# Second MLP product by seven block products, with four sums a side instead of five and the combination done by accumulating in PSUM

## The chip, the cores and the metric

The kernel runs on one core of a Trainium2 chip. The metric is the device time of one execution in microseconds (us). A run also records the core's span from its first to its last instruction, which is some 1.8 us shorter than the time, and the mean granted clock of TensorE.

Names: PE is TensorE (matmuls), PEld its weight loads, DVE is VectorE, ACT is ScalarE, POOL is GpSimd, SP is the queue that issues most transfers. PSUM is the memory that matmuls write; the kernel has eight buffers in it, called banks here, each of the size of one matmul result of 128 x 512 in fp32. L587 means line 587 of that kernel; the same code has other line numbers before and after the change.

## The reference

Causal attention with decay, in blocks of 64 positions, and behind it an MLP with a gelu:

```python
for b in range(nb):                       # B=4, H=8, S=768, D=64; block 64
    intra = (qb @ kb.T * Dmask) @ vb
    inter = (qb * lam_pow) @ kv_state
    out[:, :, sl] = intra + inter
    kv_state = lam_block * kv_state + (kb * rev_pow).T @ vb
x = out.transpose(0, 2, 1, 3).reshape(B * S, H * D)       # 3072 x 512
h = x @ w_in                                              # 512 x 2048
g = 0.5 * h * (1 + tanh(c * (h + 0.044715 * h**3)))
return g @ w_out                                          # 2048 x 512
```

The change concerns the last line alone, `g @ w_out`.

## The kernel before

Attention runs in 24 steps. The MLP's work lies in a list `filler`, from which pieces are taken between the parts of the attention steps, so that TensorE always has something to do. The rows of the MLP go in seven groups: g = 0 has 512 rows and takes plain products, g = 1 and 2 have 256 rows, g = 3 to 6 have 512. From g = 1 on the second product splits activations and weights into 2 x 2 blocks and makes seven block products in place of eight. A block product is eight matmuls of 256 columns. The blocks are combined by sums on both sides (VectorE), and the products by adds (VectorE) behind copies (ScalarE):

```python
G_SUMS = {5: ((0, 0), ALU.add, (0, 1)), 2: ((1, 0), ALU.add, (1, 1)),
          1: ((0, 0), ALU.add, (1, 1)), 7: ((0, 1), ALU.subtract, (1, 1)),
          6: ((1, 0), ALU.subtract, (0, 0))}
PLACE = {4: ("A", 0), 3: ("A", 1), 5: ("B", 0), 2: ("B", 1), 1: ("C", 0), 7: ("D", 0), 6: ("D", 1)}

def product(m, p):
    ...
    for i in range(HF):
        ...
        pin(nc.tensor.matmul(dst, lhsT, rhs, start=(i == 0), stop=(i == HF - 1),
                             skip_group_check=True))
    if m == 2:
        ...
        pin(nc.scalar.activation(out=m525[:, 0:2], in_=B[:], func=AF.Copy))
        pin(nc.scalar.activation(out=m525[:, 2], in_=B[:, 0], func=AF.Copy))
        pin(tt(banks["diag"], A[:], m525[:, 0:2], ALU.subtract))
        pin(tt(flat[:, 1:3], A[:], m525[:, 1:3], ALU.add))
    elif m == 1:
        pin(tt(d, banks["C"][:, 0].unsqueeze(1).to_broadcast([P, 2, HE]), d, ALU.add))
    elif m == 6:
        pin(tt(d, banks["D"][:], d, ALU.add))
        # then two stores of 256 KB; in the last pair four of 128 KB, each as soon as it can go
```

Each product writes its half of a bank once and no product waits for a read in the middle of its own bank's life. `pin` keeps the program's order on each engine.

## Time and profile before

| what | value | where from |
|---|---|---|
| time | 204.34 us, median of 5 (203.80 to 204.52) | the runs |
| span of the profiled run | 202.2 us | the page |
| busy: PE, DVE, ACT | 194.2, 145.7, 107.9 us | the page, part 1 |
| PE in the chain that ended last | 81% | the page, part 4 |
| granted clock | 1.000 | the view of cores |
| last matmul starts, span ends | 198.54, 202.16 us | the trace |

The lines themselves stand in the prediction. Read them in this order. The busy table tells which engine has no room (PE) and which has some (DVE at 72%). The slices tell whether that holds throughout or only on average: DVE is at 9 tenths in eight slices in a row before the middle of the run and at 2 to 7 in its last fifth. The chain tells what the end waited for. Since a busy PE may still be slow, the last reading is the distance from one matmul's start to the next: 109 ns for 256 columns is its rate here, and anything above that is a hole. The holes are the only thing that a change can win back which leaves the matmuls alone.

### The profile page before, as it was taken

The page shows a single profiled execution, that of the slowest core. Times are in us where ns is not written, and L with a number is a line of the kernel's source. Part 1 is how long each engine was busy: PE and PEld are TensorE (multiplying, and loading weights), DVE is VectorE, ACT ScalarE, POOL GpSimd, SP SyncE. Part 2 cuts the span into 40 slices and gives each one's busy share as a digit, 9 for nine tenths or more (in the row PEclk, how much of TensorE's full clock was granted, in tenths as well). Part 3 has the DMA queues.
Part 4 walks back from the last instruction along what each step waited for, and adds up shares of the span by engine and source line. Part 5 has one row for each costly group of instructions (what it writes and reads, how often), then busy time and mean ns, then how long its engine had stood idle before and what let it go on. Part 6 is the DMA issues. An engine that isn't in the chain of part 4 may idle for free.

```text
span 202.2 us, 5666 instructions
## 1 busy us (share of the span) xinstructions
PE 194.2 (96%) x2348; PEld 130.1 (64%) x2348; DVE 145.7 (72%) x293; ACT 107.9 (53%) x205; POOL 66.3 (33%) x80
## 2 busy tenths in 40 slices
PE   6888999999999999999999999999999999999993
PEld 1456544456888888645688764589664688544882
DVE  5896623889999999967799749899566462334753
ACT  2475778375893473477642368614367424466210
POOL 6594123457458264162531609303302000000000
PEclk9999999999999999999999999999999999999999
DMA  5999999999999999999875999306510003300014
GB/s 170 291 327 387 387 387 378 286 291 320 334 239 216 272 233 235 210 277 200 205 182 127 243 285 218 45 0 138 132 51 3 0 0 107 104 0 0 3 45 163
DMA packets 64201, 37.85 MB, mean 187 GB/s; under 512 B 17584, under 2 KB 59568, under 8 KB 64176
## 3 DMA queue, kind: packets, MB, share of 16 engines
q1 hardware_dynamic: 63344, 36.97, 72.1%
q10 hardware_dynamic: 832, 0.52, 0.8%
q8 instruction: 18, 0.29, 0.6%
q14 instruction: 7, 0.06, 0.1%
HBM read 27.26 MB, written 6.29 MB: 166 GB/s over the span
## 4 chain that ended last, share of the span: by engine, by line
PE 81%; DVE 6%; SPq 4%; DMA 4%; ACT 2%; issue 2%; DVEq 0%
PE Hps L484 37%; PE MB L555 8%; PE MA L555 8%; PE MD L555 7%; SPq L70 4%; PE MC L555 4%; DMA wi<-in_moe_w_in_dram 4%; PE Hps L601 3%; PE O2ps L499 3%; PE S L295 3%; DVE w_sum L128 2%; PE OK L353 2%; PE OK L344 1%; PE Tps L266 1%; DVE gs L531 1%
## 5 line engine op out<-in xcount | busy, mean ns | idle before, releaser
L484 PE MATMUL Hps<-xT,w_in 128*128 128x512 f16 (+1 forms) x416 | 78.7, 346 | 0.0
L488 ACT ACTIVATE gT<-Hps 128x512 f16<-128x512 f32 x88 | 52.3, 597 | 29.1 <-PE Hps L484 28.3
L484 PEld LDWEIGHTS <-w_in 128*128 128x128 f16 x416 | 40.4, 98 | 33.7
L531 DVE TENSOR_TENSOR gs<-gT 128x1024 f16<-128x1024 f16 (+1 forms) x62 | 40.8, 712 | 18.3 <-ACT gT L488 18.3
L456 POOL TENSOR_TENSOR u<-t,lumask 128x256 f16<-128x256 f32 x40 | 29.4, 749 | 67.0 <-DVE t L449 49.6
L555 PEld LDWEIGHTS <-gs 128*128 128x128 f16 x400 | 39.0, 98 | 4.5
L305 DVE TENSOR_TENSOR PT<-S,mask 128x512 f16<-128x512 f32 x48 | 30.4, 682 | 9.5 <-PE S L295 9.5
L230 POOL TENSOR_TENSOR v<-v,dv 128x512 f16<-128x512 f32 x24 | 28.5, 1194 | 5.0 <-DMA v<-in_v_dram 4.5
L555 PE MATMUL MA<-w_sum,gT 128*128 128x256 f16 x160 | 19.5, 273 | 0.4 <-DVE o L587 0.3
L555 PE MATMUL MB<-w_out,gs 128*128 128x256 f16 x160 | 19.1, 273 | 0.0
L248 ACT ACTIVATE qk<-k 128x512 f16<-128x512 f32 x24 | 15.0, 625 | 7.6 <-DMA k<-in_k_dram 7.6
L562 ACT ACTIVATE m<-MB 128x512 f32<-128x512 f32 x10 | 6.0, 597 | 23.4 <-PE MB L555 23.4
L555 PE MATMUL MD<-w_sum,gs 128*128 128x256 f16 x152 | 18.4, 273 | 0.0
L555 PEld LDWEIGHTS <-gT 128*128 128x128 f16 x160 | 15.4, 98 | 3.5 <-ACT gT L488 0.5
L243 DVE TENSOR_TENSOR qk<-q,dq 128x512 f16<-128x512 f32 x23 | 17.6, 767 | 0.0
L430 ACT ACTIVATE xT<-OK 128x256 f16<-128x256 f32 x29 | 11.1, 453 | 8.2 <-PE OK L353 7.9
L499 PE MATMUL O2ps<-w_out,gT 128*128 128x512 f16 x64 | 14.6, 379 | 0.0
L566 DVE TENSOR_TENSOR o<-MA,m 128x512 f32<-128x512 f32 x10 | 6.9, 689 | 9.6 <-ACT m L562 9.6
L128 DVE TENSOR_TENSOR w_sum<-w_out 128x1024 f16<-128x1024 f16 x10 | 9.1, 947 | 6.3 <-POOL w_out L118 3.5
L430 ACT ACTIVATE xT<-O 128x256 f16<-128x256 f32 x18 | 6.4, 458 | 10.4 <-PE O L404 7.5
L295 PEld LDWEIGHTS <-qkT 64*64 64x64 f16 x384 | 6.0, 106 | 7.0 <-issue 3.2
L449 DVE SCALAR_TENSOR_TENSOR t<-t,lamu,OK 128x64 f32<-128x64 f32 x44 | 10.1, 273 | 0.5
(68 smaller groups left out, 168.8 us busy)
## 6 DMA issues: line engine op xcount, KB each, us to landing
q<-in_q_dram SPq DMA_DIRECT2D x24, 256.0 KB, 5.3
k<-in_k_dram SPq DMA_DIRECT2D x24, 256.0 KB, 5.2
v<-in_v_dram SPq DMA_DIRECT2D x23, 256.0 KB, 5.2
out_dram<-o SPq DMA_DIRECT2D x22, 256.0 KB, 4.5
wo<-in_moe_w_out_dram SPq DMA_DIRECT2D x4, 1024.0 KB, 9.6
wi<-in_moe_w_in_dram SPq DMA_DIRECT2D x4, 512.0 KB, 7.6
wi<-in_moe_w_in_dram SPq DMA_DIRECT2D x2, 1024.0 KB, 12.7
v<-in_v_dram ACTq DMA_DIRECT2D x1, 256.0 KB, 4.4
```

The source lines that it names most:

```text
L128: pin(eng.tensor_tensor(w_sum16[:, w_slot[m], 4 * j : 4 * j + 4, :], rows(f0, e0), rows(f1, e1), op))
L230: pin(nc.gpsimd.tensor_tensor(wide(tv[:]), ld32[s][2][:], decay(dv, s), ALU.mult))
L243: pin(q_eng.tensor_tensor(wide(tq), q32[:], decay(dq, s), ALU.mult))
L248: pin(nc.scalar.activation(out=wide(tk), in_=k32[:], func=AF.Copy))
L305: pin(nc.vector.tensor_tensor(t[:, hl].rearrange("p b c d -> p b (c d)"), Sps[:].rearrange("p b c d -> p b (c d)"), mask[:].unsqueeze(1).t ...
L430: pin(nc.scalar.activation(out=d, in_=o, func=AF.Copy))
L456: pin(nc.gpsimd.tensor_tensor(u[:], state[half][:].unsqueeze(2).to_broadcast([P, 2, 2, D]), lumask[:, 2 * half : 2 * half + 2, :].unsqueez ...
L484: pin(nc.tensor.matmul(by_block(Hps[:, i, :]), w_in16[:, c, f * P : (f + 1) * P], x(c), start=(c == 0), stop=(c == NC - 1)))
L488: pin(nc.scalar.activation(out=dst, in_=Hps[:], func=AF.Gelu_apprx_tanh))
L499: pin(nc.tensor.matmul(O2[tau][0][:], gT[:, f % HF, f // HF, tau * P : (tau + 1) * P], w_out16[:, f, :], start=(n == 0), stop=(n == NF - 1)))
L531: pin(nc.vector.tensor_tensor(gsum[m][:, i, :], block(T0, F0, i), block(T1, F1, i), op))
L555: pin(nc.tensor.matmul(dst, lhsT, rhs, start=(i == 0), stop=(i == HF - 1), skip_group_check=True))
```

## The change

With activation blocks Gij (i: half of the rows, j: half of the 2048) and weight blocks Wij, the new form is

```
S1 = G10+G11   S2 = S1-G00   S3 = G00-G10   S4 = G01-S2
T1 = W01-W00   T2 = W11-T1   T3 = W11-W01   T4 = W10-T2
P1 = G00*W00  P2 = G01*W10  P3 = S4*W11  P4 = G11*T4  P5 = S1*T1  P6 = S2*T2  P7 = S3*T3
out00 = P1+P2   out01 = P1+P6+P5+P3   out11 = P1+P6+P7+P5   out10 = P1+P6+P7+P4
```

Its intent is to take work off VectorE: four sums a side instead of five, and a combination that TensorE does itself by accumulating. Bank X takes products 1, 6, 7 and 4 one upon the other and is read between them; W takes product 2; Y takes 5 and then 3. The order is 1 2 5 6 3 7 4, for both row tiles of a group in turn. The price is that some sums are now made from other sums (S2 from S1, S4 from S2), and that TensorE has to wait until a bank has been read before it may go on in it. Each sum is issued by itself, behind a chosen product. Core of the diff:

```diff
-        G_SUMS = {5: ((0, 0), ALU.add, (0, 1)), ... five of them, each of two plain blocks
+        G_SUMS = {1: ((1, 0), ALU.add, (1, 1)), 2: (1, ALU.subtract, (0, 0)),
+                  3: ((0, 0), ALU.subtract, (1, 0)), 4: ((0, 1), ALU.subtract, 2)}
+        FACTORS = {1: ((0, 0), (0, 0)), 2: ((0, 1), (1, 0)), 3: (4, (1, 1)), 4: ((1, 1), 4),
+                   5: (1, 1), 6: (2, 2), 7: (3, 3)}
...
+        paired = HN // P == 2                     # groups of 512 rows
...
+                if m == 1:
+                    st["X"] = ps_M.tile([P, HE], FP32, tag="M", name="MX")[:]
+                elif m == 2 and paired:
+                    wy = ps_M.tile([P, 2, HE], FP32, tag="M", name="MWY")
+                    st["W"], st["Y"] = wy[:, 0], wy[:, 1]
...
+            opens = m in (1, 2) or (m == 5 and not paired)
+            closes = m in (2, 3, 4)
...
+            if m == 1:
+                copied("m1")                      # ScalarE, from X
+            elif m == 2:
+                added(0, 0, "m1")                 # VectorE, W + m1
+            elif m == 5:
+                copied("q")                       # ScalarE, from Y
+            elif m == 6:
+                copied("u2")                      # ScalarE, from X
+            elif m == 3:
+                added(1, 0, "u2")                 # VectorE, Y + u2
+                store(0)
+            elif m == 7:
+                added(1, 1, "q")                  # VectorE, X + q
+                if final:
+                    store(1, 1)
+            elif m == 4:
+                pin(nc.scalar.activation(out=o[:, 0, 1, :], in_=dst, func=AF.Copy))
+                store(1, 0 if final else None)
...
-        ms = ((3, 4, 5, 2), (1, 7, 6))
+        order = [(m, p) for m in (1, 2, 5, 6, 3, 7, 4) for p in range(HN // P)]
...
+            behind(5, 0, 4, (1, 2))
+            behind(6, 0, 4, (4, 3))
+            behind(7, 4, 8, (1,))
+            behind(8, 4, 8, (2,))
+            behind(9, 4, 8, (4,))
+            behind(10, 4, 8, (3,))
...
+    BURST = {18: (2, 5, 4), 20: (3, 10, 5), 22: (3, 6, 4)}
+    for n, (a, b, c) in BURST.items():
+        burst((n, n + 1), (17,) if n == 18 else (n - 2, n - 1))
+        fill(a)
+        U(n)                                      # state updates: VectorE, then GpSimd
+        U(n + 1)
+        if n + 3 < NSTEP:
+            prep(n + 3)                           # q scaling on VectorE, and more
+        fill(b)
...
```

The weight sums follow the same pattern (eight instructions instead of ten), and steps 16 and 17, which were one burst, become two single steps.

More of the change, by code (lines that the diff above doesn't have):

```diff
@@ L78 @@
     HF, HE = NF // 2, DM // 2
-    w_sum16 = w16p.tile([P, 5, HF, HE], FP16)
-    W_SUMS = {3: ((0, 1), ALU.subtract, (1, 1)), 4: ((1, 0), ALU.subtract, (0, 0)),
-              1: ((0, 0), ALU.add, (1, 1)), 7: ((1, 0), ALU.add, (1, 1)),
-              6: ((0, 0), ALU.add, (0, 1))}
+    w_sum16 = w16p.tile([P, 4, HF, HE], FP16)
+    W_SUMS = {1: ((0, 1), ALU.subtract, (0, 0)), 2: ((1, 1), ALU.subtract, 1),
+              3: ((1, 1), ALU.subtract, (0, 1)), 4: ((1, 0), ALU.subtract, 2)}
     w_slot = {m: i for i, m in enumerate(W_SUMS)}
@@ L120, in sum_wout, with rows @@
     def sum_wout(j, m, eng):
-        (f0, e0), op, (f1, e1) = W_SUMS[m]
-        def rows(f, e):
-            f = f * HF + 4 * j
-            return w_out16[:, f : f + 4, e * HE : e * HE + HE]
-        pin(eng.tensor_tensor(w_sum16[:, w_slot[m], 4 * j : 4 * j + 4, :], rows(f0, e0), rows(f1, e1), op))
+        a, op, b = W_SUMS[m]
+        r = slice(4 * j, 4 * j + 4)
+        def rows(t):
+            if t in w_slot:
+                return w_sum16[:, w_slot[t], r, :]
+            f, e = t
+            return w_out16[:, f * HF + r.start : f * HF + r.stop, e * HE : e * HE + HE]
+        pin(eng.tensor_tensor(rows(m), rows(a), rows(b), op))
     lam_in = const.tile([H, 1], FP32)
@@ L460, in update, with gs_tiles @@
             us[(s, c)] = u
+    gs_kept = []
+    def gs_tiles(g):
+        if g < 3:
+            if not gs_kept or gs_kept[0] != g:
+                gs_kept[:] = [g, wst.tile([P, 4, HF, P], FP16, tag="w32", name=f"gs_{g}")]
+        elif not gs_kept or gs_kept[0] < 3:
+            gs_kept[:] = [3] + [wst.tile([P, 2, HF, 2 * P], FP16, tag="w32", name=f"gs{i}")
+                                for i in range(2)]
+        return gs_kept[1:]
     groups = [[0, 1], [2], [3], [4, 5], [6, 7], [8, 9], [10, 11]]
@@ L510, in queue_group @@
         HN = N // 2
-        G_SUMS = {5: ((0, 0), ALU.add, (0, 1)), 2: ((1, 0), ALU.add, (1, 1)),
-                  1: ((0, 0), ALU.add, (1, 1)), 7: ((0, 1), ALU.subtract, (1, 1)),
-                  6: ((1, 0), ALU.subtract, (0, 0))}
-        G_PLAIN = {3: (0, 0), 4: (1, 1)}
-        W_PLAIN = {5: (1, 1), 2: (0, 0)}
-        gsum, pairs = {}, []
-        def block(T, F, i):
+        G_SUMS = {1: ((1, 0), ALU.add, (1, 1)), 2: (1, ALU.subtract, (0, 0)),
+                  3: ((0, 0), ALU.subtract, (1, 0)), 4: ((0, 1), ALU.subtract, 2)}
@@ L519, in block, with g_rows, sum_g @@
+        FACTORS = {1: ((0, 0), (0, 0)), 2: ((0, 1), (1, 0)), 3: (4, (1, 1)), 4: ((1, 1), 4),
+                   5: (1, 1), 6: (2, 2), 7: (3, 3)}
+        gsum = {}
+        def g_rows(t, i):
+            if t in G_SUMS:
+                return gsum[t][:, i, :]
+            T, F = t
             return gT[:, i, F, T * HN : (T + 1) * HN]
-        def sum_g(i0, i1, ms=None):
-            for m, ((T0, F0), op, (T1, F1)) in G_SUMS.items():
-                if ms and m not in ms:
-                    continue
+        def sum_g(i0, i1, ms):
+            for m in ms:
+                a, op, b = G_SUMS[m]
@@ L525, in sum_g @@
                 if m not in gsum:
                     k = len(gsum)
-                    if k % 2 == 0:
-                        pairs.append(wst.tile([P, 2, HF, HN], FP16, tag="w32", name=f"gs_{g}_{m}"))
-                    gsum[m] = pairs[-1][:, k % 2]
+                    held = gs_tiles(g)
+                    gsum[m] = held[0][:, k] if per == 2 else held[k // 2][:, k % 2]
                 i = slice(i0, i1)
-                pin(nc.vector.tensor_tensor(gsum[m][:, i, :], block(T0, F0, i), block(T1, F1, i), op))
+                pin(nc.vector.tensor_tensor(g_rows(m, i), g_rows(a, i), g_rows(b, i), op))
@@ L533, in queue_group @@
+        last_group = g == len(groups) - 1
+        paired = HN // P == 2
         of_pair = {}
-        PLACE = {4: ("A", 0), 3: ("A", 1), 5: ("B", 0), 2: ("B", 1), 1: ("C", 0), 7: ("D", 0),
-                 6: ("D", 1)}
-        def product(m, p):
-            banks = of_pair.setdefault(p, {})
-            name, half = PLACE[m]
-            final = g == len(groups) - 1 and p == HN // P - 1
-            if final and m == 6:
-                name = "E"
-            if m in (3, 5, 1, 7) or name == "E":
-                banks[name] = ps_M.tile([P, 2, HE], FP32, tag="M", name=f"M{name}")
-            dst = banks[name][:, half]
-            t = slice(p * P, p * P + P)
-            for i in range(HF):
-                lhsT = block(*G_PLAIN[m], i)[:, t] if m in G_PLAIN else gsum[m][:, i, t]
-                if m in W_PLAIN:
-                    F, E = W_PLAIN[m]
-                    rhs = w_out16[:, F * HF + i, E * HE : E * HE + HE]
-                else:
-                    rhs = w_sum16[:, w_slot[m], i, :]
-                pin(nc.tensor.matmul(dst, lhsT, rhs, start=(i == 0), stop=(i == HF - 1),
-                                     skip_group_check=True))
-            tt = nc.vector.tensor_tensor
-            if m == 2:
-                o = banks["o"] = otp.tile([P, 2, 2, HE], FP32, tag="o32", name="o32")
-                A, B = banks["A"], banks["B"]
-                m525 = mtp.tile([P, 3, HE], FP32, tag="m525", name="m525")
-                pin(nc.scalar.activation(out=m525[:, 0:2], in_=B[:], func=AF.Copy))
-                pin(nc.scalar.activation(out=m525[:, 2], in_=B[:, 0], func=AF.Copy))
-                flat = o[:].rearrange("p e t d -> p (e t) d")
-                banks["diag"] = flat[:, 0:4:3]
-                pin(tt(banks["diag"], A[:], m525[:, 0:2], ALU.subtract))
-                pin(tt(flat[:, 1:3], A[:], m525[:, 1:3], ALU.add))
-                if final:
-                    for T, queue in ((1, nc.sync), (0, nc.scalar)):
-                        row = row0 + T * HN + p * P
-                        E = slice((1 - T) * HE, (1 - T) * HE + HE)
-                        pin(queue.dma_start(out=out[row : row + P, E], in_=o[:, 1 - T, T, :]))
-            elif m == 1:
-                d = banks["diag"]
-                pin(tt(d, banks["C"][:, 0].unsqueeze(1).to_broadcast([P, 2, HE]), d, ALU.add))
-            elif final and m in (7, 6):
-                o, T = banks["o"], (0 if m == 7 else 1)
@@ new lines, in product, with copied, added, store @@
+        def product(m, p, part=None):
+            st = of_pair.setdefault(p, {})
+            if part != 1:
+                if m == 1:
+                    st["X"] = ps_M.tile([P, HE], FP32, tag="M", name="MX")[:]
+                    st["o"] = otp.tile([P, 2, 2, HE], FP32, tag="o32", name="o32")
+                elif m == 2 and paired:
+                    wy = ps_M.tile([P, 2, HE], FP32, tag="M", name="MWY")
+                    st["W"], st["Y"] = wy[:, 0], wy[:, 1]
+                elif m == 2:
+                    st["W"] = ps_M.tile([P, HE], FP32, tag="M", name="MW")[:]
+                elif m == 5 and not paired:
+                    st["Y"] = ps_M.tile([P, HE], FP32, tag="M", name="MY")[:]
+            dst = st[{2: "W", 5: "Y", 3: "Y"}.get(m, "X")]
+            opens = m in (1, 2) or (m == 5 and not paired)
+            closes = m in (2, 3, 4)
+            a, b = FACTORS[m]
+            for i in range(HF) if part is None else range(HF // 2 * part, HF // 2 * part + HF // 2):
+                lhsT = g_rows(a, i)[:, p * P : p * P + P]
+                if b in W_SUMS:
+                    rhs = w_sum16[:, w_slot[b], i, :]
+                else:
+                    F, E = b
+                    rhs = w_out16[:, F * HF + i, E * HE : E * HE + HE]
+                pin(nc.tensor.matmul(dst, lhsT, rhs, start=(opens and i == 0),
+                                     stop=(closes and i == HF - 1), skip_group_check=True))
+            if part == 0:
+                return
+            o = st["o"]
+            def copied(name):
+                t = mtp.tile([P, HE], FP32, tag=f"{name}{p}", name=f"{name}_{p}")
+                pin(nc.scalar.activation(out=t[:], in_=dst, func=AF.Copy))
+                st[name] = t[:]
+            def added(E, T, name):
+                pin(nc.vector.tensor_tensor(o[:, E, T, :], dst, st[name], ALU.add))
+            def store(T, E=None, queue=nc.sync):
@@ L579, in product @@
                 row = row0 + T * HN + p * P
                 rows = out[row : row + P, :].rearrange("q (e d) -> q e d", e=2)
-                d = o[:, T, T, :]
-                pin(tt(d, banks[name][:, half], d, ALU.add))
-                queue = nc.scalar if m == 7 else nc.sync
-                pin(queue.dma_start(out=rows[:, T], in_=d))
-            elif m == 6:
-                d = banks["diag"]
-                pin(tt(d, banks["D"][:], d, ALU.add))
-                for T in range(2):
-                    row = row0 + T * HN + p * P
-                    pin(nc.sync.dma_start(out=out[row : row + P, :].rearrange("q (e d) -> q e d", e=2),
-                                          in_=banks["o"][:, :, T, :]))
+                E = slice(0, 2) if E is None else E
@@ new lines, in store @@
+                pin(queue.dma_start(out=rows[:, E], in_=o[:, E, T, :]))
+            final = last_group and p == HN // P - 1
+            if m == 1:
+                copied("m1")
+            elif m == 2:
+                added(0, 0, "m1")
+            elif m == 5:
+                copied("q")
+            elif m == 6:
+                copied("u2")
[9 more added lines that the diff above has]
+                store(1, 0 if final else None)
@@ L626, in queue_group, with behind @@
                 filler.append(lambda fs=fs: mm1(fs))
-        ms = ((3, 4, 5, 2), (1, 7, 6))
-        order = [(m, p) for p in range(HN // P) for m in ms[0] + ms[1]]
-        if g == len(groups) - 1:
-            order = [(m, p) for part in ms for p in range(HN // P) for m in part]
+        order = [(m, p) for m in (1, 2, 5, 6, 3, 7, 4) for p in range(HN // P)]
         for m, p in order:
             filler.append(lambda m=m, p=p: product(m, p))
-        def behind(k, i0, i1, ms=None):
+        def behind(k, i0, i1, ms):
             piece = filler[at + k]
@@ L646, in queue_group @@
         if per == 2:
-            behind(5, 0, 4, (5, 2))
-            behind(7, 4, 8, (5,))
+            behind(5, 0, 4, (1, 2))
+            behind(6, 0, 4, (4, 3))
+            behind(7, 4, 8, (1,))
             behind(8, 4, 8, (2,))
-            behind(9, 0, 8, (1, 7))
-            behind(10, 0, 8, (6,))
-        else:
-            behind(9, 0, 4)
-            behind(13, 4, 6, (5, 2))
-            behind(n1 - 1, 6, 8, (5,))
-            behind(n1, 6, 8, (2,))
-            behind(n1 + 1, 4, 8, (1, 7))
-            behind(n1 + 2, 4, 8, (6,))
+            behind(9, 4, 8, (4,))
+            behind(10, 4, 8, (3,))
+        else:
+            behind(9, 0, 4, (1, 2, 4, 3))
+            behind(n1, 4, 8, (1,))
+            behind(n1 + 1, 4, 8, (2,))
+            behind(n1 + 2, 4, 8, (4,))
+            behind(n1 + 4, 4, 8, (3,))
     def fill(n):
@@ L746 @@
     cast_wout(3, (POOL, ACT))
-    for m in (6, 3, 4, 1, 7):
+    for m in W_SUMS:
         sum_wout(0, m, DVE)
-    sum_wout(1, 6, DVE)
+    sum_wout(1, 1, DVE)
     fill(9)
@@ L753 @@
     prep(5)
-    sum_wout(1, 3, DVE)
+    sum_wout(1, 2, DVE)
     fill(2)
@@ L764 @@
     prep(7)
-    sum_wout(1, 4, DVE)
+    sum_wout(1, 3, DVE)
     fill(2)
@@ L772 @@
     stage_t(7)
-    sum_wout(1, 1, DVE)
-    sum_wout(1, 7, DVE)
+    sum_wout(1, 4, DVE)
     fill(2)
@@ L779 @@
     fill(2)
-    for n in range(8, 16):
+    FILL = {8: (0, 2, 1, 2), 9: (2, 2, 1, 2), 10: (0, 1, 1, 3), 11: (0, 2, 1, 2), 12: (0, 2, 1, 3),
+            13: (0, 2, 1, 3), 14: (0, 3, 1, 3), 15: (0, 2, 1, 3), 16: (0, 2, 1, 3), 17: (0, 3, 1, 3)}
+    for n, (a, b, c, d) in FILL.items():
         stage_t(n)
-        fill(1 if n == 9 else 0)
+        fill(a)
         prep_qk(n + 2) if n == 8 else prep(n + 2)
-        fill({9: 1, 14: 3}.get(n, 2))
+        fill(b)
         R(n, n - 1)
-        fill(1)
+        fill(c)
         U(n)
@@ L790 @@
             prep_v(n + 2)
-        fill(2 if n in (8, 11, 15) else 3)
-    prep(18)
-    fill(2)
-    for n in range(16, NSTEP, 2):
-        burst((n, n + 1), (15,) if n == 16 else (n - 2, n - 1))
-        fill(2)
+        fill(d)
+    prep(20)
+    BURST = {18: (2, 5, 4), 20: (3, 10, 5), 22: (3, 6, 4)}
+    for n, (a, b, c) in BURST.items():
+        burst((n, n + 1), (17,) if n == 18 else (n - 2, n - 1))
+        fill(a)
         U(n)
         U(n + 1)
-        for m in (n + 3, n + 4):
-            if m < NSTEP:
-                prep(m)
-            fill(4 if m % 2 == 0 and n % 4 == 0 else 6 if m % 2 == 0 else 6 if n % 4 == 0 else 10)
+        if n + 3 < NSTEP:
+            prep(n + 3)
+        fill(b)
+        if n + 4 < NSTEP:
+            prep(n + 4)
+        fill(c)
     burst((), (NSTEP - 2, NSTEP - 1))
```

## The prediction

> **What bounds the kernel now.** First the page's busy table and its slices.
>
> ```profile
> span 202.2 us, 5666 instructions
> PE 194.2 (96%) x2348; PEld 130.1 (64%) x2348; DVE 145.7 (72%) x293; ACT 107.9 (53%) x205; POOL 66.3 (33%) x80
> PE   6888999999999999999999999999999999999993
> DVE  5896623889999999967799749899566462334753
> PEclk9999999999999999999999999999999999999999
> PE 81%; DVE 6%; SPq 4%; DMA 4%; ACT 2%; issue 2%; DVEq 0%
> ```
>
> TensorE (PE) is busy from the fifth slice to the end at a full granted clock, and the chain that ended last is 81% PE. Busy alone does not say that the matmuls stream at their rate, so next the same chain in order of time:
>
> ```profile
> 39.08 0.61 DVE qk L243
> 39.74 0.62 PE Tps L266 x8
> ...
> 107.29 0.70 DVE o L587
> 108.03 1.91 PE MA L555 x16
> 109.94 1.75 PE MB L555 x16
> 111.68 0.87 PE MC L555 x8
> ```
>
> A product of eight 256-column matmuls takes 0.87 us, 109 ns each, and sixteen take 1.75: the second MLP product runs at one matmul per 109 ns. I compared the start-to-start distances of all matmuls in the trace with that rate. From 39 us on only four holes exceed 0.15 us: 0.33 us at 39.2 us (a transpose waits for VectorE's scaling of q, behind five weight sums), 0.17 at 69.8, about 0.3 at 75.6 (a late gelu) and 0.5 at 107.5 us (bank MA waits for the add at L587; the first and last are in the lines above, where the chain passes from VectorE to PE). So at most some 1.3 us of 202 can be gained by anything that does not take matmuls away.
>
> **What the Trainium skill says.** "TensorE: Matmul & The Clock Gate", section "Back-to-back issue gap": a warm matmul of N columns takes N/2.4 + 2.5 ns; for 256 that is 109.2, and the trace agrees (109). "PSUM — Partial Sum Buffer", section "PSUM bank collisions raise a hardware error": a matmul writing and VectorE or ScalarE reading one bank at once is an error even at disjoint columns, so access must be ordered by bank, not by address. No wait of the kernel before shows it, but it decides the change. "SBUF — State Buffer", section "Who interferes with whom": a VectorE instruction with two SBUF inputs contends with a GpSimd instruction that reads SBUF. The trace agrees: the 128x1024 sums from 176 to 190 us, with GpSimd idle, average 0.69 us (starts 0.60 to 0.62 apart), and the four from 123 to 128 us, while GpSimd scales v, average 1.21 us.
>
> **The change, part by part.**
>
> ```profile
> L531 DVE TENSOR_TENSOR gs<-gT 128x1024 f16<-128x1024 f16 x38 | 29.6, 836 | 9.7 <-ACT gT L488 9.7
> L531 DVE TENSOR_TENSOR gs<-gT 128x512 f16<-128x512 f16 x24 | 11.6, 516 | 8.7 <-ACT gT L488 8.7
> L128 DVE TENSOR_TENSOR w_sum<-w_out 128x1024 f16<-128x1024 f16 x10 | 9.1, 947 | 6.3 <-POOL w_out L118 3.5 <-ACT w_out L116 2.8
> L582 DVE TENSOR_TENSOR o<-ME,o 128x256 f32<-128x256 f32 x1 | 0.4, 426 | 0.4 <-PE ME L555 0.4
> L563 ACT ACTIVATE m<-MB 128x256 f32<-128x256 f32 x10 | 3.8, 377 | 0.0
> ```
>
> TensorE: still seven products of eight 256-column matmuls per pair of row tiles, ten pairs; 560 matmuls before and after. Nothing removed. One burst (two attention steps together) becomes two single steps: before, the bursts of steps 16 and 18 take 1.43 and 1.82 us; after, two single steps of about 0.97 and a burst of about 1.45 make 3.4. Cost 0.15 us.
>
> VectorE: weight sums 10 to 8, less 2 x 0.95 = 1.9 us. Activation sums: five to four a group, so from 38 large and 24 small to 32 and 16, less 6 x 0.84 + 8 x 0.52 = 9.1 us. Combining a pair: four adds of 512 columns at about 0.685 become three of 256 at 0.426, less 1.46 us a pair, 14.6 for ten. Together 25.6 us of 145.7. ScalarE: copies of 512 and 256 columns (0.597 + 0.377) become four of 256 (1.51), plus 5.3 us of 107.9. Neither sets the end, so this is worth only the holes it closes: one of five weight sums (3.33/4 = 0.83 us) goes ahead of the q scaling, which closes the 0.33 us hole, and the 0.5 us hole at L587 goes with its add and its burst. Gain 0.8 us. At the end, a 0.38 us copy stands for a 0.43 us add before the last store, with 256 KB less stored just ahead of it: gain 0.1.
>
> What is added are TensorE waits on evacuations inside the accumulation. Reading the waits built into the changed program: bank X is copied after products 1 and 6 and read after 7, before TensorE may go on in it. One product of 0.875 us or more lies in between; the tightest case is 7 to 4 in the paired groups, where only the other tile's product does and VectorE has the work. From the end of the run:
>
> ```profile
> 197.78 1.04 PE L555 MATMUL ME<-w_sum,gs 128*128 128x256 f16 x8
> 198.85 0.43 DVE L582 TENSOR_TENSOR o<-ME,o 128x256 f32<-128x256 f32 x1 [0.45 <-PE ME L555]
> ```
>
> The last matmul starts at 198.54, the add 0.31 us later, takes 0.43, and PE follows a VectorE end by 0.05 (107.99 to 108.03): 0.79 us against 0.109 + 0.875 = 0.98. It just fits if VectorE is free, and at 7 to 4 its queue is. In the two small groups an attention step lies there.
>
> The dangerous pair is W and Y of the paired groups: two halves of one bank. Product 5 opens Y while W is still to be read, so its first matmul waits, by bank, for the add that reads W after product 2, again with 0.875 us in between. VectorE's queue is in order, and between the adds of the two tiles stand a sum, and where the filler is cut there, state updates and a q scaling. The costs of these in a burst of before:
>
> ```profile
> 119.01 2.48 DVE L305 TENSOR_TENSOR PT<-S,mask 128x512 f16<-128x512 f32 x4 [3.38 <-PE S L295]
> 121.41 0.48 DVE L446 COPY t<-K 128x128 f32<-128x128 f32 x2
> 121.81 0.85 DVE L449 SCALAR_TENSOR_TENSOR t<-t,lamu,K 128x64 f32<-128x64 f32 x4
> 122.57 0.94 DVE L243 TENSOR_TENSOR qk<-q,dq 128x512 f16<-128x512 f32 x1
> ```
>
> The fifth group (g = 4) meets the burst of steps 20 and 21. From the burst's start: PE 1.63 for the burst, then products 1, 1, 2, 2 until 5.13. VectorE: masks from 0.45 to 2.8, four updates to 3.6, two sums with GpSimd's state masks beside them (0.6 to 1.2 each) to about 5.5, the add of W0 to 5.9, a sum to 6.5, four updates to 7.3, the q scaling to 8.2, the add of W1 to 8.6. Product 5 of tile 0 waits from 5.13 to 5.95 (0.8), and of tile 1 from 6.8 to 8.65 (1.8). Together 2.6 us.
> The fourth group (g = 3) is cut by a single step; the same count gives tile 0 nothing and tile 1 0.6 us (one sum and two updates between the adds). In the last two groups only a sum of 0.6 stands there: about 0.1 for both.
>
> Sum: -0.8 - 0.1 + 0.15 + 2.6 + 0.6 + 0.1 = +2.5 us. I shade that to +2.0, since the filler counts look tuned for this order and the contended sums are the softest term: 206.3 us.
>
> **The rivals.** First, VectorE's 25.6 us show in the time: a gain of 3 to 5 us, near 200. For it: VectorE is 90% busy or more in fourteen slices. Against: the chain has it at 6%, nearly all in its queues ahead of the two holes at 39 and 107 us, and PE has no others worth filling. Second, the adds of W come in time and only the closed holes count: 203.4 us. For it: the tuned cuts; against: the order of VectorE's queue is fixed. Third, the bank waits are worse, because the masks or sums of the burst start late, or because a transposed q/k load for step 19, now queued behind the group's first stores and with some 6 us to land (3.1 to 6.5 in before), comes after its burst: one to two us more, up to 208.5. Fourth, ScalarE's four copies come late behind gelus: little, as the copies come after the gelus of their group, and have 1.75 us and more.
>
> **Range and chances.** The floor is the second rival, less noise: 203.3; the top is the third, less its tail: 208.2. Faster by 2% needs 200.3, which no hole pays for: 0.01. Slower by 2% needs 208.4, the sum with all soft terms high: 0.07. Within 2%: 0.92.
>
> **What would show it.** Right: VectorE busy near 120 us, ScalarE near 113, PE's group time unchanged; in the list of waits, matmuls of bank MWY waiting for the add of o, 2 to 4 us in total, the longest near 1.8 us just after the burst of steps 20 and 21; holes at 39 and 107 us gone. Wrong: no such waits (then rival two), or waits of matmuls on ScalarE's copies, on MX after product 7, or of scores on the transposed loads.

## The result, and the profile after

The time after is 207.25 us, the median of five runs (207.22 to 208.84), against 204.34. The ratio is 1.0158, with a 95% interval from 1.0122 to 1.0193. Here and below a ratio is the mean time of one kernel's runs over that of the other's of the same rounds, so it is not quite the ratio of the medians quoted. Executions over 1.5% slower than the fastest of the same kernel are left out of the means. The kernel is slower by 1.6%, which counts as the same at 2%; 206.3 with 203.3 to 208.2 had been predicted.

The profile was taken on the slowest of the five runs (208.84 us). The page of the kernel after, its span, busy table, three rows of slices and the chain's shares:

```profile
span 207.0 us, 5693 instructions
PE 195.8 (95%) x2348; PEld 130.6 (63%) x2348; DVE 125.1 (60%) x266; ACT 114.3 (55%) x225; POOL 65.9 (32%) x80
PE   6888999999999999999999999959999999999992
DVE  5896624789998589278785499881165233031630
PEclk9999999999999999999999999988999999999999
PE 83%; DVE 5%; SPq 4%; DMA 4%; issue 2%; ACT 1%; DVEq 0%; ACTq 0%
```

VectorE lost 20.6 us of work and has room nearly everywhere, and the time did not fall. What is new in PE's row is one slice at 5 tenths, the 27th, from 134.6 to 139.7 us. And the clock row has 8 in that slice and in the next. The waits of the kernel after (engine, bank, line, who released it: us in total, times, longest) have one line that has next to no match before (there, one wait of 0.3 us of bank MA for an add):

```profile
PE MWY L575 <- DVE o L587: 2.8, 3, 1.6
```

Start to start, the three holes are 0.59 us at 103.9 us (g = 3), 0.95 at 134.7 and 1.75 at 136.6 (g = 4), together 3.28 us. They are somewhat longer than the waits listed, since the list counts from the modelled end of the matmul ahead. VectorE's timeline in g = 4 shows why (start, us, engine, line, operation, out<-in):

```profile
133.44 0.94 DVE L544 TENSOR_TENSOR gs<-gT 128x1024 f16<-128x1024 f16 x1
134.41 0.98 DVE L544 TENSOR_TENSOR gs<-gs,gT 128x1024 f16<-128x1024 f16 x1
135.32 0.41 DVE L587 TENSOR_TENSOR o<-MWY,m 128x256 f32<-128x256 f32 x1
135.66 0.67 DVE L544 TENSOR_TENSOR gs<-gT,gs 128x1024 f16<-128x1024 f16 x1
136.25 0.84 DVE L451 SCALAR_TENSOR_TENSOR t<-t,lamu,K 128x64 f32<-128x64 f32 x4
137.02 1.00 DVE L245 TENSOR_TENSOR qk<-q,dq 128x512 f16<-128x512 f32 x1
137.94 0.41 DVE L587 TENSOR_TENSOR o<-MWY,m 128x256 f32<-128x256 f32 x1
```

The two lines of L587 are the adds that read W, for tile 0 and tile 1. The first stands behind two sums, the second behind a sum, four updates and a scaling of q. All that time VectorE is never idle, and TensorE stands still, because product 5 writes Y, the other half of the bank that the add has yet to read. The chain that ended last (start, us, engine, group) has both ends of the story:

```profile
31.95 7.77 PE O2ps L512 x36
39.72 0.45 PE Tps L268 x8
...
138.02 0.34 DVE o L587
138.40 1.87 PE MWY L575 x8
140.27 2.38 PE MX L575 x16
142.65 1.75 PE MWY L575 x16
```

At 39 us the chain no longer leaves PE: the first hole of before is closed, and the one at 107 us is closed too (of the smaller two, that at 69.8 is gone and that at 75 stays). At 138 us the chain passes through the add. And there is something that was not predicted: sixteen matmuls of MX take 2.38 us and the sixteen after them 1.75. In the trace, 13 matmuls from 138.6 to 141.2 us start 214 ns apart instead of 109. The clock did that; the view of stretches (stretch, length, busy of each engine with PE first, then the granted clock, the transfers' share and GB/s) has it:

```profile
134.61:138.03 3.42, 1.43 (x12) 0.97 (x11) 3.42 (x9) 0.38 (x1) 1.41 (x3) 1.00 0.00 0
138.03:141.44 3.41, 3.04 (x15) 2.18 (x15) 1.00 (x2) 0.38 (x1) 1.90 (x2) 0.50 0.41 77
```

The traces also tell when this happens. In them the granted clock changes only at boundaries that lie whole multiples of 3.41 us apart (here it was full for 133.1 us, 39 of them, then half for one, then full for 64.9, 19 of them). Counted from its first change to full clock, the twelve traces hold 693 such stretches. In ten of them PE is busy for 1.45 us or less, and after each of these ten the clock is half (four in mid-kernel, six at the end of a run); in the other 683 PE is busy for 1.7 us or more, and the clock stays full. So here it was the idle time within one stretch that counted, and the boundaries fall differently against the holes from run to run.

The other four runs of this kernel had a clock of 0.998 or more and took 207.22 to 207.46 us; the profiled one had 0.990. So the profile shows a cost of some 1.5 us, by the starts of its matmuls, that the median does not contain. Finally the end. The timeline of before, its last stores (SPq and ACTq are the issuing queues), and of after:

```profile
196.95 1.22 SPq L590 DMA_DIRECT2D out_dram<-o  x2
198.43 0.35 ACTq L584 DMA_DIRECT2D out_dram<-o  x1
199.30 0.36 SPq L584 DMA_DIRECT2D out_dram<-o  x1
```

```profile
199.10 4.73 SPq L593 DMA_DIRECT2D out_dram<-o  x5
203.00 0.38 ACT L612 ACTIVATE o<-MX 128x256 f32<-128x256 f32 x1 [0.54 <-PE MX L575]
```

Before, the last store is of 128 KB, issued at 199.30, and the one ahead of it (128 KB) at 198.43. After, it is issued at 203.47, and the one ahead of it, at 202.48, has 256 KB. From the start of the last matmul to the end of the span it is 3.62 us before and 4.40 after.

The profiled difference in the last matmul's start, 202.64 − 198.54 = 4.10 us, is made up so: 3.28 for the three holes; 1.46 for the clock (24 matmuls take 4.08 us from the start at 138.40, where 2.62 is their rate); 0.15 for a later beginning (the first matmul of `O2ps` starts at 31.79 us instead of 31.64); and a gain of 0.79 that is left over. Own banks, below, shows the same 0.79. It is the closed holes (0.33, 0.17 and 0.5, together 1.0) less some 0.2 for what the new order adds; of that, the two single steps (0.15 in the prediction) were not measured apart.

### The profile page after: what moved, and what is told of

It reads as the page before. It is cut to its first block, busy times and chain, and to the rows that moved or that the text cites. A ratio compares the mean times of both kernels' runs of the same rounds, so it can differ in the third digit from the quotient of the medians.

```text
span 207.0 us, 5693 instructions
## 1 busy us (share of the span) xinstructions
PE 195.8 (95%) x2348; PEld 130.6 (63%) x2348; DVE 125.1 (60%) x266; ACT 114.3 (55%) x225; POOL 65.9 (32%) x80
## 4 chain that ended last, share of the span: by engine, by line
PE 83%; DVE 5%; SPq 4%; DMA 4%; issue 2%; ACT 1%; DVEq 0%; ACTq 0%
PE Hps L497 36%; PE MX L575 16%; PE MWY L575 8%; PE O2ps L512 7%; SPq L70 4%; DMA wi<-in_moe_w_in_dram 4%; PE Hps L623 3%; PE S L297 3%; PE OK L355 2%; DVE PT L307 2%; PE MY L575 2%; PE OK L346 2%; PE Tps L268 1%; DVE t L451 1%; DVE gs L544 1%
## 5 line engine op out<-in xcount | busy, mean ns | idle before, releaser
L575 PEld LDWEIGHTS <-gs 128*128 128x128 f16 x320 | 32.0, 100 | 7.6 <-issue 3.3
L544 DVE TENSOR_TENSOR gs<-gT 128x1024 f16<-128x1024 f16 (+1 forms) x24 | 17.9, 745 | 23.3 <-ACT gT L501 23.3
L575 PEld LDWEIGHTS <-gT 128*128 128x128 f16 x240 | 23.1, 98 | 3.7 <-ACT gT L501 0.5
L575 PE MATMUL MX<-w_sum,gs 128*128 128x256 f16 x160 | 20.1, 279 | 0.0
L432 ACT ACTIVATE xT<-OK 128x256 f16<-128x256 f32 x33 | 12.7, 453 | 8.8 <-PE OK L355 8.6
L512 PE MATMUL O2ps<-w_out,gT 128*128 128x512 f16 x64 | 14.6, 379 | 0.0
L612 ACT ACTIVATE o<-MX 128x256 f32<-128x256 f32 x10 | 3.8, 383 | 17.6 <-PE MX L575 17.6
L575 PE MATMUL MWY<-w_sum,gs 128*128 128x256 f16 x64 | 8.8, 290 | 2.8 <-DVE o L587 2.8
L587 DVE TENSOR_TENSOR o<-MWY,u 128x256 f32<-128x256 f32 x8 | 3.4, 424 | 12.9 <-PE MWY L575 12.9
L583 ACT ACTIVATE q<-MWY 128x256 f32<-128x256 f32 x8 | 3.1, 383 | 13.9 <-PE MWY L575 11.8
L512 PEld LDWEIGHTS <-gT 128*128 128x128 f16 x64 | 6.1, 98 | 6.6
L575 PE MATMUL MX<-w_out,gT 128*128 128x256 f16 x80 | 10.2, 273 | 0.1
```

Of the source, the lines that this page charges most:

```text
L432: pin(nc.scalar.activation(out=d, in_=o, func=AF.Copy))
L512: pin(nc.tensor.matmul(O2[tau][0][:], gT[:, f % HF, f // HF, tau * P : (tau + 1) * P], w_out16[:, f, :], start=(n == 0), stop=(n == NF - 1)))
L544: pin(nc.vector.tensor_tensor(g_rows(m, i), g_rows(a, i), g_rows(b, i), op))
L575: pin(nc.tensor.matmul(dst, lhsT, rhs, start=(opens and i == 0), stop=(closes and i == HF - 1), skip_group_check=True))
```

## The experiments

Ten kernels ran; each is compared with runs of the kernel before on the same chip. Edits are relative to the changed kernel. All outputs were correct. The theory to test: the gain on VectorE is worth nothing because VectorE did not set the end; the loss is the wait for the shared bank, and a longer end. The main rivals: VectorE's total matters after all, or the loss comes from the new order or from the clock.

### W and Y in banks of their own

```diff
-        paired = HN // P == 2
+        paired = False
```

> The sums W and Y of a pair of row tiles get a bank each in the large groups (as they have in the small ones); order of all queues unchanged. Theory (the waits of product 5 for the add that reads W come from the shared bank): the three holes of 0.59, 0.95 and 1.75 us in the TensorE stream vanish, 3.3 us less than the changed kernel, about 203.9 to 204.3 us, ratio to before 0.998 to 1.003, and no stretch at lower clock. Rival (the VectorE queue is late there anyway and something else of it, the sums or the state updates, would stop TensorE next): at most 1 us less, 206 us or more. Rival (a seventh and eighth bank in use makes attention wait for banks): new waits of S, OK or Hps matmuls of 1 us or more.

Measured: 204.27 us median of six (203.75 to 205.67), before 203.79; ratio 1.0031 [1.0000, 1.0062]. Nothing in TensorE's list waits for an add of W any more. PE's timeline of this kernel where the long holes were:

```profile
132.20 1.91 PE L575 MATMUL MW<-w_out,gT 128*128 128x256 f16 x16
133.94 1.91 PE L575 MATMUL MY<-w_sum,gs 128*128 128x256 f16 x16
```

Products 2 and 5 of both tiles follow each other without a hole, although VectorE's queue holds the same instructions in the same order: here the second add of W ends at 137.46 us, some 2.6 us after product 5 of that tile began (133.94 plus one product of 0.87). So the late add costs nothing unless the bank is shared. This one line removes 3.0 us of the median (2.4 if each is taken against the kernel before of its own call). It also gives the worth of the closed holes: the last matmul starts at 197.59, against 198.54 before, of which 0.16 is an earlier beginning (31.48 and 31.64 us) and 0.79 the holes, while the end takes 4.39 us like the changed kernel's.

### The adds ahead of the updates

The cut after the burst of steps 20 and 21 comes one piece later, so that the second add of W goes ahead of the updates and the scaling of q:

```diff
-    BURST = {18: (2, 5, 4), 20: (3, 10, 5), 22: (3, 6, 4)}
+    BURST = {18: (2, 5, 4), 20: (4, 9, 5), 22: (3, 6, 4)}
```

> One filler piece is moved: in the fifth group product 2 of the second row tile, and so its add of W, comes ahead of the state updates and the q scaling of steps 20 to 23 instead of behind them. Bank still shared. Theory (the length of a wait is what VectorE's queue holds between the adds of the two tiles): the 1.75 us wait falls to 0 to 0.3 us, the 0.95 and 0.59 us waits stay, time 1.5 to 1.8 us under the changed kernel, about 205.6 us, ratio 1.006. Rival (a wait for the bank itself, whatever the queue): no change, 207.2 us.

Measured: 206.06 us (205.49 to 207.21), ratio 1.0110 [1.0082, 1.0137]. The holes at 103.7 us (0.59) and 134.6 (0.95) stay, the one of 1.75 is gone. The median fell by 1.2 us, less than the 1.5 to 1.8 expected; in the trace the whole hole is gone. The size of the wait is what stands ahead of the add in VectorE's queue.

### Product 6 before product 5

```diff
-        order = [(m, p) for m in (1, 2, 5, 6, 3, 7, 4) for p in range(HN // P)]
+        ms = (1, 2, 6, 5, 3, 7, 4) if paired else (1, 2, 5, 6, 3, 7, 4)
+        order = [(m, p) for m in ms for p in range(HN // P)]
```

> In the large groups product 6 goes ahead of product 5 (order 1 2 6 5 3 7 4), so that two products of 0.875 us more lie between product 2 and the first matmul that must wait for the add of W. Bank still shared. Theory: in the fifth group the add of W0 (ready at 135.7 us in the changed kernel's trace) is in time, the add of W1 is late by some 0.3 us, and product 6 waits 0 to 0.5 us for the second half of its sum; the fourth group's 0.59 us wait goes. Together 2.2 to 3 us less, 204.3 to 205 us, ratio 1.000 to 1.004. Rival (the slack does not matter): 207 us.

Measured: 205.23 us (204.87 to 206.57), ratio 1.0075 [1.0047, 1.0104]. The banks stay shared, but product 6 of both tiles now lies between W's last matmuls and Y's first. Two holes are left, 0.18 us at 135.5 (product 6) and 0.76 at 137.9 (product 5 of tile 1, again behind the add). The direction is as expected and the time just outside the range given; the second add came later than I had put it, by half a microsecond. Together the four kernels make a scale:

| kernel | holes for the shared bank, us | median, us | above the first row |
|---|---|---|---|
| own banks | 0 | 204.27 | 0 |
| product 6 first | 0.94 | 205.23 | 0.96 |
| adds ahead | 1.54 | 206.06 | 1.79 |
| the change as it is | 3.28 | 207.25 | 2.98 |

A microsecond of hole is about a microsecond of time. The last row ran in an earlier call, where the kernel before took 204.34 instead of 203.79; less that difference it is 2.4 above, and in the repetition told below 3.0 (207.99 and 204.52).

### The last stores cut smaller

```diff
             elif m == 7:
                 added(1, 1, "q")
-                if final:
+                if last_group:
                     store(1, 1)
             elif m == 4:
                 ...
-                store(1, 0 if final else None)
+                store(1, 0 if last_group else None, nc.scalar if final else nc.sync)
```

The store of tile 0, of 256 KB just ahead of the last, goes as two of 128 KB, the first of them earlier; the very last goes through ACT's queue.

> In the last group the second row half of the first tile is stored in two parts, as for the last tile, and the very last store is issued by ScalarE, so that only 128 KB go ahead of the last 128 KB instead of 256. From the last matmul's start to the end the changed kernel takes 4.40 us and the kernel before 3.62. Theory (the last store queues behind the 256 KB store issued 1.0 us before it): 0.4 to 0.8 us less, 206.4 to 206.9 us. Rival (the end is a matter of ScalarE against VectorE, or of the run): no change, within 0.2 us of 207.25. The waits for bank MWY stay, 3.3 us.

Measured: 207.90 us (206.29 to 209.77), ratio 1.0184 [1.0133, 1.0235], "unclear", and no faster than the change. The end is shorter, 3.63 us from the last matmul's start in place of 4.40. But three of six runs had a clock of 0.992 and took 208.82, 209.06 and 209.77 (the last counts as slow); the three at 0.999 or more took 206.29, 206.53 and 206.99. The profiled run was one of the latter; the view of its stretches:

```profile
134.70:138.12 3.42, 1.73 (x15) 1.25 (x13) 3.39 (x9) 0.38 (x1) 1.41 (x3) 1.00 0.00 0
138.12:141.53 3.41, 2.74 (x26) 2.45 (x26) 1.31 (x3) 0.77 (x2) 2.21 (x2) 1.00 0.41 77
```

The holes are the same three, yet the clock is full: the boundary falls 0.67 us before the end of the long hole, where in the changed kernel's profile it fell 0.37 before it, so PE is busy for 1.73 us of the stretch instead of 1.43. The same holes sometimes bring the clock down and sometimes not, and this experiment settles the stores by the trace, not by its median.

### Own banks, every activation sum twice

```diff
-                pin(nc.vector.tensor_tensor(g_rows(m, i), g_rows(a, i), g_rows(b, i), op))
+                for _ in range(2):
+                    pin(nc.vector.tensor_tensor(g_rows(m, i), g_rows(a, i), g_rows(b, i), op))
...
-        paired = HN // P == 2
+        paired = False
```

> Own banks for W and Y as in e1, and every sum of activations is issued twice on VectorE (the second overwrites the first with the same values), which adds 48 instructions, some 24 us of VectorE time, so it is as busy as in the kernel before. Theory (VectorE's total is off the path; only what stands in its queue ahead of a needed add counts): within 0.6 us of e1, 204.0 to 204.9 us, with small waits of product 5 or 6 for the second half of a sum. Rival (VectorE's relief is what made e1 equal to before): 2 us or more over e1, 206.3 us and up.

Measured: 220.84 us (219.41 to 221.97), ratio 1.0803: a miss by 16 us. VectorE is busy 156.5 us, more than before's 145.7, and TensorE waits for the sums themselves. The two largest lines of its waits:

```profile
PEld L576 <- DVE gs L545: 10.0, 6, 2.8
PE MY L576 <- DVE gs L545: 6.0, 4, 2.5
```

I had taken VectorE's total for the thing tested. But the sums stand one right ahead of its product, and S4 needs S2, which needs S1: doubled, they lengthen a chain that leads straight into TensorE. This run does not tell whether a load on VectorE that is well ahead of its product would have been free. The clock was 0.964 to 0.992 in it.

### Own banks, and stores cut smaller

The edits of the first and the fourth experiment together.

> e1 and e4 together: own banks, and the last stores in smaller parts with the very last on ScalarE's queue. Theory (the two are independent terms: 3.3 us of holes and 0.8 us of end): 0.8 us under e1, 203.2 to 203.7 us, ratio to before 0.995 to 1.000; from the last matmul's start to the end 3.5 to 3.7 us. Rival (e4's end was chance): 204.2 us.

Measured: 203.77 us (203.28 to 204.59), before 204.52; ratio 0.9965 [0.9937, 0.9994]. All clocks 0.997 or more. The end takes 3.62 us. With both faults mended the change is as fast as before or a little faster.

### The same, with one gelu earlier

The hole at 75 us, which is left from before, waits for a gelu; one piece of filler goes ahead of the preparation of step 13.

```diff
-    ... 11: (0, 2, 1, 2), ...
+    ... 11: (1, 1, 1, 2), ...
```

> e6, and in the third group one filler piece (the last first-layer matmuls of that group) is issued ahead of the scaling of q and k of step 13, so that its gelu stands ahead of the copy of k in ScalarE's queue. Theory (the hole of 0.33 us at 75 us is that order): the hole goes, 0.3 us under e6, 202.9 to 203.4 us. Rival: the hole moves to the attention step that needs step 13 or stays, no gain.

Measured: 203.51 us (203.28 to 204.10), ratio 0.9954 [0.9929, 0.9980]. The hole at 75 us is gone, one of 0.15 us is left at 66 us. The difference to the kernel without this edit, 0.26 us, is inside the scatter of both. This is the best version found, 0.5% under the kernel before.

### The change again

> The changed kernel unaltered, on the same chip as the three others, for comparison with e1 to e4. Theory: 207.2 us, ratio to before 1.014 to 1.018, the three waits of 0.59, 0.95 and 1.75 us again and the same 4.4 us end; if this execution keeps the full clock, the span is about 205.4 us, if the clock drops after the holes, 207.

Measured, on chip 0 like the three kernels above (the first four ran on chip 5): 207.99 us (207.24 to 209.65), before 204.52, ratio 1.0186 [1.0146, 1.0225], "unclear" at 2%. The holes are 0.59, 0.95 and 1.75 us once more. Two of six runs had a clock of 0.990 and 0.991 and took 209.43 and 209.65; four had 0.999 or 1.000 and took 207.24 to 208.04. The profile fell on one of the two, and 15 matmuls in it start 213 to 214 ns apart. Over the three kernels with all holes (the change twice, and the one with smaller stores), 6 of 17 runs had 0.990 to 0.992 and 11 had 0.998 or more. Over the six kernels timed without the hole of 1.75 us and without doubled sums, none of 36 runs was below 0.996. The drop costs 1.6, 1.7 and 2.5 us by the medians of the runs with and without it in those three sets; 3.41 us at half clock can cost 1.7 at most, so the rest of the 2.5 is scatter.

### Own banks, only the early sums twice

After the miss above, only the sums of the first half (issued well ahead of their products) were doubled:

```diff
+                for _ in range(2 if i0 == 0 else 1):
```

> Own banks as in e1; only the sums of the first half of a group's columns (issued some five microseconds before any product needs them) are issued twice, none of those that follow a group's last gelu. It adds 24 instructions, 12 to 16 us of VectorE time. Theory (VectorE's total is off the path; e5 was slow because its copies stood ahead of sums that products waited for): no TensorE hole over 0.5 us, within 0.8 us of e1, 204.0 to 205.0 us. Rival (any added VectorE work shows): 5 us or more over e1, as half of what e5 added, 209 us and up.

Measured: 210.01 us (208.75 to 211.31), before 203.82; ratio 1.0300 [1.0264, 1.0336], 5.7 us above the kernel with own banks. A miss again, and the rival came true. VectorE is busy 142.5 us, 3 us less than in the kernel before, which has next to no holes; here are seven of 0.3 to 1.3 us, 4.7 in all. Its timeline on VectorE at the first of them, then PE's:

```profile
62.11 1.28 DVE L307 TENSOR_TENSOR PT<-S,mask 128x512 f16<-128x512 f32 x2
...
63.69 0.42 DVE L545 TENSOR_TENSOR gs<-gT 128x512 f16<-128x512 f16 x1
```

```profile
64.16 0.61 PE L576 MATMUL MY<-w_sum,gs 128*128 128x256 f16 x4 [1.09 <-DVE gs L545]
```

With own banks alone, the masks start at 59.14 and this sum at 60.72; here they start three microseconds later, of which 1.4 was there from the beginning (first matmul of `O2ps` at 32.86 and 31.48 us). The sums of the first half are early for their own products, but VectorE's queue is in order, so everything behind them moves, and the sums of the second half, which stand right ahead of product 5, come too late for it. What can be concluded: taking work off VectorE won little by itself (own banks is no faster than before, and its gain ahead of the end is the 0.79 us of the closed holes), but the new order, with sums made from sums and placed late, needs the room that this left.

### Stores cut smaller, on the same queue

The kernel with own banks and smaller stores, but with the very last store on SP like the others:

```diff
-                store(1, 0 if last_group else None, nc.scalar if final else nc.sync)
+                store(1, 0 if last_group else None)
```

> e6 without the change of queue: own banks, the last group's second row half of the first tile stored in two parts, all stores from the same queue. Tells which of e6's two edits shortens the end. Theory (the 256 KB store just ahead is what delays the last one): from the last matmul's start to the end 3.6 to 3.8 us as in e6, 203.3 to 203.9 us. Rival (the queue it is issued from): 4.4 us as in the changed kernel, 204.3 us.

Measured: 203.70 us (203.10 to 204.04), before 203.82; ratio 0.9990 [0.9967, 1.0013]. The last matmul starts at 197.75 and the span ends at 201.34, 3.60 us later. So the shorter end comes from the smaller store ahead, and the other queue adds nothing that one profile of each shows (3.62 and 3.60). This agrees with what the Trainium skill says in "DMA: Bandwidth & Descriptors", section "Issuing engines are not separate DMA queues": transfers run on the same engines whoever issues them, so an issue from elsewhere only saves time on the sequencer.

## Why the prediction was right, and where it was off

The prediction held: 207.25 lies in the range, and the class was right. It was low by 0.95 us. By its own steps:

- **The bank of W and Y** (0.8 + 1.8 in g = 4, 0.6 in g = 3, about 0.1 in the last two groups). Measured 0.95, 1.75, 0.59 and nothing: 3.28 in place of 3.3. The count of VectorE's queue was right to a tenth: with the burst at 129.81 us, the two adds end 5.9 and 8.5 us after it, where 5.9 and 8.6 were written. Own banks, adds ahead and product 6 first each remove the waits that they should, and the scale of four kernels shows that the time follows them.
- **The two closed holes** (−0.8). Both are gone in the trace. With the early scatter taken off, the kernel with own banks gains 0.79 us up to its last matmul; that includes a third small hole, 0.17 us at 69.8, and what the new order adds.
- **The end** (−0.1). This is the step that failed: "At the end, a 0.38 us copy stands for a 0.43 us add before the last store, with 256 KB less stored just ahead of it". The copy was right, but the store just ahead did not shrink; tile 0's second row half now leaves whole, 256 KB, one microsecond before the last 128 KB. The end took 0.78 us more in place of 0.1 less. Cutting that store brings it to 3.60 us, as short as before.
- **The shading** (+2.5 to +2.0) had no measured reason, and without it the prediction would have been 206.8. With the end at +0.78 the sum is +3.4; the medians differ by 2.9, and the scatter of single runs is of that size.
- **The clock** was not in the prediction. In about a third of the runs with all three holes, TensorE ran its matmuls at half rate after the long hole, for 2.8 and 3.2 us in the two traces that have it. The median of the first five runs contains none of this, and that is luck: one of the five had the drop, and with three of five the median would have been near 208.8, above the range. The condition is shown by the 693 stretches and not by an experiment: PE busy for 1.45 us or less of 3.41. Moving the boundaries over the holes of the three traces, I estimate that 23% of the positions meet that, and that 40% lie at or under 1.72, the lowest that kept the full clock; 6 of 17 runs, 35%, had the drop. Why those two limits are where they are stays open.
- **Rival one**, VectorE's saved time shows as a gain: refuted by the kernel with own banks, which keeps the whole relief and is not faster than before; all that the relief can have bought is in the closed holes. But the sentence that neither VectorE nor ScalarE sets the end was too simple. It is true of the changed kernel as it stands. It is not true of the new order with a VectorE as loaded as before, as the two kernels with doubled sums show.
- **Rival two**, only the closed holes count, 203.4 us: this is what own banks with the end mended gives, 203.70 and 203.77. **Rival three and four**, late loads or late copies: one weight load of the scores waits 0.4 us for a transfer, at 114.4 us, with no hole in the matmuls (own banks has it too); no matmul of MX waits for a copy.
- **Sizes on VectorE**: 125.1 us busy in place of 120. The adds came out as written (27.5 to 12.5 us, so −15.0 against −14.6), and the weight sums (−2.0 against −1.9). The activation sums lost 5.4 us instead of 9.1: the small ones now average 0.63 us where 0.52 was taken over from before. ScalarE, 114.3, met its 113. The four contended sums that the prediction averages to 1.21 us took 0.69, 1.10, 1.53 and 1.52; the first began beside GpSimd's state masks, and only the third and most of the fourth lie beside the scaling of v, so that average mixes two cases.

## What to carry to other kernels

When products accumulate in a bank that is read between them, give each running sum a bank of its own as long as banks are free, or else follow the in-order queue of the engine that reads it and see what stands ahead of the read. Relief on an engine that does not set the end buys little by itself, but a new order may live on it, so test that with the load put back where it was, not only by the totals. Count the bytes stored in the last microseconds from the issues in the trace. Look at the clock of each run before taking one profile for the kernel, and add up neighbouring holes of TensorE, since here two that fell into one stretch of 3.41 us brought the clock down together.

## What the Trainium skill lacked or had wrong

- "TensorE: Matmul & The Clock Gate", section "HAM oscillation — how this bites in real kernels", tells of half clock after a gap of more than about 3.4 us; of shorter gaps the page says that frequent ones between groups of matmuls can do it too, but not how much idle time is enough. Here two gaps of 0.95 and 1.75 us, with 0.87 us of matmuls between them, were followed by 13 to 15 matmuls at 213 to 214 ns instead of 109, in 2 of the 3 profiles with these gaps; runs of those kernels with a clock of 0.990 to 0.992 were 6 of 17. Kernels whose longest gap was 0.95 us (adds ahead) and 1.26 us (early sums twice) kept 0.996 or more in all runs. In all twelve traces, 1.45 us or less of busy PE in a stretch of 3.41 us was followed by half clock, and 1.7 us or more was not.
- The same page, section "Back-to-back issue gap", gives about 131 ns per matmul as the sustained figure for 512 columns and calls its formula too high there. In this kernel eight matmuls of 512 columns take 1.73 us in the chain of before, 216 ns each, which is the formula's value.
- "SBUF — State Buffer", section "Who interferes with whom", says that a sum of two SBUF inputs contends with GpSimd, but not by how much: in the profile of before, a sum of 128x1024 took 0.69 us alone, and 1.53 and 1.52 us beside GpSimd's scaling of v.
- No page tells what a store just ahead costs the last one: 256 KB instead of 128 KB one microsecond before the last 128 KB made the end 4.40 us long instead of 3.60.
